# A retention layer and a swish MLP on one core: all crossbar transposes on the SyncE queue, batch 2's among them, and eight stores held back

## The chip, the core and the metric

The kernel runs on one core of a Trainium2 chip. Its time is the device time of one execution in microseconds (us). Times of single steps come from one profiled execution, counted from the start of its span.

## What is computed

Eight batches of eight heads (sequence 576, head size 64) go through a retention layer, attention without softmax whose scores are weighted by a decay per head, and then through an MLP with a swish whose slope beta is given per hidden unit.

```python
scores = (q @ k.T) / sqrt(64)                       # q, k, v: 8 x 8 x 576 x 64, float32
D      = where(i >= j, gamma[h] ** (i - j), 0)      # gamma[h] = 1 - 2 ** (-5 - h)
x      = ((scores * D) @ v)                         # heads side by side: 4608 x 512
h      = x @ w_in                                   # 512 x 2048
out    = (h / (1 + exp(-beta * h))) @ w_out         # 2048 x 512, out 4608 x 512 float32
```

## The kernel before

**Tiles.** A batch's first 512 rows are cut into four chunks of 128. The last 64 rows of two batches together make a tail tile of 128, so there are four of these. The list `seq` numbers the tiles in the order of their attention: 0 to 15 are the chunks of batches 0 to 3, 16 and 17 two tails, 18 to 33 batches 4 to 7, 34 and 35 the other two tails. The MLP works in blocks of 512 rows: block m below 8 holds the first 512 rows of batch m, block 8 all the tails.

**The order.** Everything is written in the order in which each engine is to run it. `fill` is a list of MLP steps: `up` (L406; 4 matmuls of 512 columns and a Silu on ScalarE) and `down` (L419; 4 matmuls and, after four of them, an eviction to `ot` by VectorE and a store on SyncE's DMA queue, called SP here, L436). `streams` are lists of attention steps with a due place each, and `merged` (L443) puts a step ahead of the first fill step whose number has reached its due place. `d0` = 16 and `u1` = 32 are the places where block 0's down projection and block 1's up projection begin; block 1's down projection begins at step 58; `base[2]` = 74 is the start of block 2's up projection, and each later block takes 32 steps.

**The attention of one tile.** `load_q` (L74) and `load_kv` (L85) fetch q of a batch, and k and v of one chunk, on SP. `load_kv(n)` counts chunks without the tails. `pre_q` (L237) scales q by the decay into `qs` in bf16, and `pre` (L251) casts k to `kn` (L273) and scales v to `vn` (L255); from batch 2 on all of these run on GpSimd. q and k must then be transposed, to `qT` and `kT`. Then `first` (L542) runs the state update `a_st` and the scores `a_sc` (L323, masked by VectorE into `R`), and `outputs` (L547) the products with v (L366), those with the state (L351) and the eviction `xT` that the up projection reads.

**Two kinds of transposes.** For batches below `XB`, `t_q` (L294) and `t_k` (L300) transpose on TensorE into PSUM tiles `T` and copy them out (L298, L304). From `XB` on, `x_q` (two for a batch), `x_k` (one for two chunks) and `x_tail` (one for a tail) call `turn` (L280), a crossbar transpose by DMA from SBUF to SBUF. Before the change `turn` issues on ScalarE's queue. The due places of all of these are made in the lists of L527 to L539 for the first chunks, and by `pair_prep` (L553) for the others; the loop of L572 gives each pair of chunks the place `at` of its `first`.

An issue on SP or ScalarE waits for the data and the buffers it needs, and what stands behind it on the same engine waits too. Every DMA also takes one of eight semaphores in turn, shared between the two queues, so that a ninth is issued only when the first of them has landed.

Of the kernel before, what the change touches and what calls it, by code (L numbers as in the profile page):

```python
# [19 lines left out]
def kernel(  # L20
# [10 lines left out]
    nc = tc.nc  # L31
# [9 lines left out]
    CB = MB // P  # L41
# [25 lines left out]

    NQ = 6
    E = CB
    XB = 3  # L70
    QB = 2
    q_tiles, kv_tiles = {}, {}

# [204 lines left out]
        return t[:, 2 * p:2 * p + 2, :].rearrange("p h d -> p (h d)")  # L278

    def turn(dst, src):  # L280
        nc.scalar.dma_start_transpose(dst.rearrange("p j pr s -> p (j pr) s"), src.rearrange("p j h d -> p (j h d)"))

    def x_q(b, u):
        turn(batch[b]["qT"][:, 2 * u:2 * u + 2], batch[b]["qs"][:, 2 * u:2 * u + 2])

    def x_k(b, u):
        kn, kT = pair[b, u]
        turn(kT, kn)

    def x_tail(i):  # L290
        turn(live[i]["qkT"], live[i]["qk"])
# [122 lines left out]
                             start=(ko == 0), stop=(ko == KO - 1))  # L414
        nc.scalar.activation(gts[m][:, fo, :, w], ph, ACT.Silu, scale=beta_sb[:, fo:fo + 1])  # L415

    pos_, ots = {}, {}

    def down(m, ms, f0, fn=4, n0=0, nn=d_model):  # L419

        gT = gts[m]
        if f0 == 0:
            pos_[ms] = psum.tile([P, d_model], F32, name="po", tag="mm", bufs=3)
        po = pos_[ms]
        for fo in range(f0, f0 + fn):
            nc.tensor.matmul(po[:, :nn], gT[:, fo, ms, :], w_out_sb[:, fo, n0:n0 + nn],  # L426
                             start=(fo == 0), stop=(fo == FO - 1))
        if f0 + fn < FO:
            return
        if ms == 0:  # L430
            ots[m] = stage.tile([P, MB // P, d_model], F32, name="ot", tag="wt", bufs=4)
        ot = ots[m][:, ms, n0:n0 + nn]
        nc.vector.tensor_copy(ot, po[:, :nn])  # L433
        if m < B:
            rows = out[m * S:m * S + MB].rearrange("(s i) n -> s i n", i=CB)
            nc.sync.dma_start(rows[:, ms, n0:n0 + nn], ot)  # L436
        else:
            for x in range(2):
                r0 = (2 * ms + x) * S + MB
                nc.sync.dma_start(out[r0:r0 + TL, n0:n0 + nn], ot[x * TL:(x + 1) * TL])  # L440
# [12 lines left out]
    def F(f, *a):  # L453
        return lambda: f(*a)
# [49 lines left out]
    fill = [F(up, 0, fo) for fo in range(FO)]  # L504
    d0 = len(fill)
    fill += [F(down, 0, ms, f0) for f0 in range(0, FO, 4) for ms in range(3)]
    fill += [F(down, 0, 3, f0) for f0 in range(0, FO, 4)]

    u1 = len(fill)
    fill += [F(up, 1, fo, 2 * x, 2) for x in range(2) for fo in range(10)]  # L510
    fill += [F(up, 1, fo) for fo in range(10, FO)]
    fill += [F(down, 1, ms, f0) for ms in range(MB // P) for f0 in range(0, FO, 4)]
    base = {1: u1 + 10}
    for n, m in enumerate(blocks[2:], 2):
# [6 lines left out]
    def second(i):  # L521
        for f in (a_O, lambda j: a_cross(j, False), a_x):
# [6 lines left out]
               [(d0 - 4 + 3.3 * g, F(cast_w_out, g)) for g in range(WG)],  # L529
               [(10.3, F(load_q, 1))] + [(10.3, F(load_kv, CB + n, (j,))) for n, j in keys_first],  # L530
               [(10.4, F(load_q, 2))] + [(10.4, F(load_kv, 2 * CB + n)) for n in range(2)],
               [(d0 + 8.6, F(load_kv, 2 * CB + 2)), (d0 + 10.1, F(load_kv, 2 * CB + 3))],
               [(d0 + 7, F(pre_q, 1, n)) for n in range(4)] + [(d0 + 10.6, F(t_q, 1, 0)), (d0 + 12.6, F(t_q, 1, 1))],
               [(d0 + 8, F(pre, 4, (0,))), (d0 + 8, F(pre, 5, (0,))), (d0 + 9, F(pre, 4, (1,))), (d0 + 9, F(pre, 5, (1,))),
                (d0 + 12.7, F(t_k, 4)), (d0 + 12.8, F(t_k, 5)), (d0 + 13.8, F(a_sc, 4)), (d0 + 13.81, F(a_sc, 5)),
                (d0 + 14.8, F(a_st, 4)), (d0 + 15.9, F(second, 4))],
# [16 lines left out]
    def pair_prep(i, at):  # L553
        b, c = seq[i]
        if b is None:
            return [(at - 31, F(load_tail, c)), (at - 21.5, F(pre, i)), (at - 21, F(load_tail, c + 1)),
                    (at - 13, F(pre, i + 1)), (at - 12, F(x_tail, i)), (at - 9.5, F(x_tail, i + 1))]
        n, st = full.index(i), []
        if b < XB:
            if c == 0:  # L560
                st += [(at - 12 + x, F(pre_q, b, x)) for x in range(4)]
                st += [(at - 5.5, F(t_q, b, 0)), (at - 4.5, F(t_q, b, 1))]
                st += [(at - 6.5 + x / 2, F(pre, i + x)) for x in range(CB)]
            return st + [(at - 3.5, F(t_k, i)), (at - 2.5, F(t_k, i + 1))]
        if c == 0:
            st += [(at - 30, F(load_q, b))] + [(at - 20 + x, F(pre_q, b, x)) for x in range(4)]
            st += [(at - 14 + 1.5 * x, F(x_q, b, x)) for x in range(2)]
        return st + [(at - 28, F(load_kv, n)), (at - 26, F(load_kv, n + 1)), (at - 16, F(pre, i)),
                     (at - 15, F(pre, i + 1)), (at - 10.5, F(x_k, b, c // 2))]

    todo = list(range(2 * CB, len(seq), 2))
    for n in range(1, B - 1):  # L572

        take = [i for i in todo if seq[i][0] == n + 1 or n == B - 2 or seq[i] == (None, 0) and n == CB - 1]
        todo = todo[len(take):]
        lo, hi = (base[n] + 11, base[n + 1] - 12) if n == 1 else (base[n] + 3, base[n + 1] - 8)
        at = [lo + x * (hi - lo) / (len(take) - 1) for x in range(len(take))]
        if len(take) == 2 and n > 1:
            at[1] -= 6
        for i, t in zip(take, at):  # L580
            st = pair_prep(i, t) + [(t, F(first, i))]
            if seq[i][0] is None:
                st.append((t + 5, F(second, i)))
            elif seq[i][1] == 0:
                st.append((t + 2, F(a_st, i + 1)))
            else:
                st.append((t + 5, F(outputs, i - 2)))
            streams.append(st)
# [32 lines left out]
```

## Time and profile before

| | |
|---|---|
| time, median of 3 runs | 311.74 us (311.5 to 311.76) |
| the profiled execution: time, span | 311.92 us, 310.1 us |
| TensorE matmuls busy | 298.5 us, 96% |
| ScalarE, VectorE, GpSimd busy | 143.0, 106.9, 96.0 us |
| SP's DMA queue | 46.15 MB, 61.5% of the DMA engines' span |
| ScalarE's DMA queue | 6.30 MB, 13.6% of it |
| clock granted to TensorE | 0.998 |

The span runs from the first to the last instruction; the profiled execution's time is 1.8 us longer. Busy time is the time in which an engine has at least one instruction running. The share of a DMA queue is the time that its packets took, as a share of the span of all 16 DMA engines; where packets overlap, the sum in a short window can pass 1.

### The profile page before, as it was taken

Reading aid. Unit: us, or ns where it says so; the run is one execution under the profiler, and the core shown is the slowest. Engines: PE = TensorE matmul, PEld = TensorE weight load, DVE = VectorE, ACT = ScalarE, POOL = GpSimd, SP = SyncE. Lnnn points to the kernel's source line nnn. Section 1 sums busy time; section 2 is a strip of 40 time slices with the busy share of each in tenths; the row PEclk is TensorE's granted clock in tenths of the full one; section 3 lists DMA queues with packets and bytes.
Section 4 is the critical chain, followed back from the end, with each engine's and each line's share of the span. In section 5 each row is a group of like instructions: output and inputs, shape, how many; then the busy total and the mean of one; then the engine's idle time right before and its main releaser. Section 6 shows DMA issues by size and latency. Waiting matters only on the chain.

```text
span 310.1 us, 5363 instructions
## 1 busy us (share of the span) xinstructions
PE 298.5 (96%) x2144; PEld 157.8 (51%) x2177; DVE 106.9 (34%) x191; ACT 143.0 (46%) x256; POOL 96.0 (31%) x131
## 2 busy tenths in 40 slices
PE   7789999999999999999999999999999999999995
PEld 5544456775544454454554545455545444444444
DVE  7554476342531342434430434043405420010012
ACT  5567626995138412560186117711673037207700
POOL 4663026846524282254308031902420000000000
PEclk9999999999999999999999999999999999999999
DMA  8999999998989999999897697968852110031011
GB/s 207 221 355 387 380 232 273 233 257 179 202 197 162 224 189 235 218 212 198 133 234 107 136 205 207 201 115 192 196 76 37 68 70 0 17 88 34 0 70 68
DMA packets 123897, 52.79 MB, mean 170 GB/s; under 512 B 105680, under 2 KB 116320, under 8 KB 123872
## 3 DMA queue, kind: packets, MB, share of 16 engines
q1 hardware_dynamic: 98496, 46.15, 61.5%
q10 hardware_dynamic: 25376, 6.30, 13.6%
q8 instruction: 17, 0.28, 0.4%
q14 instruction: 8, 0.07, 0.1%
HBM read 36.71 MB, written 9.44 MB: 149 GB/s over the span
## 4 chain that ended last, share of the span: by engine, by line
PE 85%; DMA 6%; SPq 5%; DVE 1%; issue 1%; ACT 1%; POOL 1%; POOLq 0%
PE po L426 40%; PE ph L413 35%; DMA wt<-in_moe_w_in_dram 4%; SPq L94 3%; PE O L366 3%; PE sc L323 3%; DMA qn<-in_q_dram 2%; PE O L351 2%; PE st L396 2%; SPq L178 1%; POOL qs L247 1%; PE T L297 1%; PE T L303 1%; ACT gT L415 0%; DVE xT L384 0%
## 5 line engine op out<-in xcount | busy, mean ns | idle before, releaser
L415 ACT ACTIVATE gT<-ph,beta_sb 128x512 bf16<-128x512 f32 (+1 forms) x154 | 99.2, 659 | 86.3 <-PE ph L413 83.4
L413 PE MATMUL ph<-xT,w_in_sb 128*128 128x512 bf16 (+1 forms) x600 | 129.3, 365 | 3.2 <-DVE w_in_sb L186 0.9
L426 PE MATMUL po<-w_out_sb,gT 128*128 128x512 bf16 (+2 forms) x591 | 126.7, 368 | 1.1 <-issue 0.3
L413 PEld LDWEIGHTS <-w_in_sb 128*128 128x128 bf16 x616 | 58.7, 98 | 65.0 <-DVE w_in_sb L186 2.3
L426 PEld LDWEIGHTS <-gT 128*128 128x128 bf16 x608 | 57.1, 98 | 62.5
L333 DVE TENSOR_TENSOR R<-sc,causal 128x512 bf16<-128x512 f32 x71 | 44.3, 684 | 68.9 <-PE sc L323 68.9
L433 DVE COPY ot<-po 128x512 f32<-128x512 f32 (+2 forms) x38 | 25.0, 662 | 92.1 <-PE po L426 92.0
L255 POOL TENSOR_TENSOR vn<-kvn,gv 128x512 bf16<-128x512 f32 x32 | 33.4, 1042 | 22.8 <-DMA kvn<-in_v_dram 11.5
L247 POOL TENSOR_TENSOR qs<-qn,gq 128x512 bf16<-128x512 f32 x24 | 24.3, 1042 | 33.2 <-DMA qn<-in_q_dram 33.2
L273 POOL CAST kn<-kvn 128x512 bf16<-128x512 f32 x32 | 19.6, 612 | 47.7 <-DMA kvn<-in_k_dram 47.3
L401 ACT CAST sbd<-st 64x256 bf16<-64x256 f32 x48 | 17.4, 362 | 15.0 <-PE st L396 14.3
L384 DVE CAST xT<-O 128x512 bf16<-128x512 f32 x24 | 15.8, 688 | 19.6 <-PE O L366 9.6
L384 ACT CAST xT<-O 128x512 bf16<-128x512 f32 x11 | 6.4, 586 | 32.2 <-PE O L351 25.2
L396 PE MATMUL st<-vn,kn 128*128 128x128 bf16 x128 | 12.4, 219 | 0.2 <-POOL vn L255 0.2
L396 PEld LDWEIGHTS <-kn 128*128 128x128 bf16 x128 | 9.3, 98 | 5.0 <-issue 0.2
L366 PE MATMUL O<-R,vn 128*64 128x128 bf16 x288 | 10.7, 221 | 0.0
L323 PE MATMUL sc<-qT,kT 64*128 64x128 bf16 x256 | 10.3, 217 | 0.4 <-ACT kT L304 0.2
L366 PEld LDWEIGHTS <-vn 128*64 128x64 bf16 x288 | 8.5, 110 | 4.1 <-issue 3.6
L323 PEld LDWEIGHTS <-kT 64*128 64x128 bf16 x288 | 8.1, 94 | 3.8 <-ACT kT L304 1.5
L304 ACT COPY kT<-T 128x512 bf16<-128x512 bf16 x12 | 6.9, 586 | 4.8 <-PE T L303 4.8
L208 PE MATMUL ph<-warm 128*128 128x128 f32 (+1 forms) x24 | 7.0, 429 | 1.2 <-DVE warm L119 1.2
L186 DVE CAST w_in_sb<-wt 128x256 bf16<-128x256 f32 (+1 forms) x14 | 6.0, 476 | 5.2 <-DMA wt<-in_moe_w_in_dram 5.2
(56 smaller groups left out, 90.2 us busy)
## 6 DMA issues: line engine op xcount, KB each, us to landing
qn<-in_q_dram SPq DMA_DIRECT2D x16, 512.0 KB, 5.8
kvn<-in_k_dram SPq DMA_DIRECT2D x32, 256.0 KB, 5.9
kvn<-in_v_dram SPq DMA_DIRECT2D x32, 256.0 KB, 5.6
out_dram<-ot SPq DMA_DIRECT2D x31, 256.0 KB, 2.7
wt<-in_moe_w_out_dram SPq DMA_DIRECT2D x4, 1024.0 KB, 9.5
wt<-in_moe_w_in_dram SPq DMA_DIRECT2D x4, 512.0 KB, 7.5
wt<-in_moe_w_in_dram SPq DMA_DIRECT2D x2, 1024.0 KB, 11.8
out_dram<-ot SPq DMA_DIRECT2D x9, 128.0 KB, 2.4
```

Of the source, the lines that this page charges most:

```text
L247: e.tensor_tensor(batch[b]["qs"][:, cs, hs], q_tiles[b][:, hs, cs].rearrange("p h i d -> p i h d"), gq[:, cs, hs].unsqueeze(3).to_broadcas ...
L255: nc.gpsimd.tensor_tensor(live[i]["vn"][:], kv_tiles.pop(i)[:, 1], gains(gv, c), ALU.mult)
L273: nc.gpsimd.tensor_copy(kn[:, c % 2], t[:, 0])
L323: nc.tensor.matmul(view(sc[j][:, p, :]), L["kT"][r, p, :], rhs, start=True, stop=True, skip_group_check=True)
L333: nc.vector.tensor_tensor(R[:, j], sc[j][:], causal4[:] if i == CB - 1 else m_b, ALU.mult)
L366: nc.tensor.matmul(O[j * D:(j + 1) * D, p, :], vn[:, 2 * p + j, :], R[:, j, p, :], start=p == 0 and not (early and crossed), stop=early or ...
L384: (nc.scalar.copy if on_act else nc.vector.tensor_copy)(x, O[:])
L396: nc.tensor.matmul(st[:, p, :], heads(L["kn"], p), heads(L["vn"], p), start=(c == 0 and p == 0), stop=True, skip_group_check=True)
L413: nc.tensor.matmul(ph, w_in_sb[:, ko, fo * P:(fo + 1) * P], xts[m][:, ko, :, w], start=(ko == 0), stop=(ko == KO - 1))
L415: nc.scalar.activation(gts[m][:, fo, :, w], ph, ACT.Silu, scale=beta_sb[:, fo:fo + 1])
L426: nc.tensor.matmul(po[:, :nn], gT[:, fo, ms, :], w_out_sb[:, fo, n0:n0 + nn], start=(fo == 0), stop=(fo == FO - 1))
L433: nc.vector.tensor_copy(ot, po[:, :nn])
```

## The change

`XB` goes from 3 to 2, so batch 2 is transposed by the crossbar as batches 3 to 7 are. `turn` issues on SP instead of ScalarE, for all 28 crossbar transposes. The stores of blocks 0 and 1 are kept in a list, and `release` issues four at 4.5 steps before `base[2]` and four at 8 steps after it. The due places around batch 2 move: its `first` steps from 53 and 62 to 58 and 64.5, its casts and scalings ahead of them, the third and fourth loads of its chunks, and the loads of batch 3's second half.

```diff
-    XB = 3
+    XB = 2
...
     def turn(dst, src):
-        nc.scalar.dma_start_transpose(dst.rearrange("p j pr s -> p (j pr) s"), src.rearrange("p j h d -> p (j h d)"))
+        nc.sync.dma_start_transpose(dst.rearrange("p j pr s -> p (j pr) s"), src.rearrange("p j h d -> p (j h d)"))
...
-    pos_, ots = {}, {}
+    pos_, ots, held = {}, {}, []
+
+    def release(n):
+        for _ in range(n):
+            nc.sync.dma_start(*held.pop(0))
...
-            nc.sync.dma_start(rows[:, ms, n0:n0 + nn], ot)
+            if m < 2:
+                held.append((rows[:, ms, n0:n0 + nn], ot))
+            else:
+                nc.sync.dma_start(rows[:, ms, n0:n0 + nn], ot)
...
-               [(d0 + 8.6, F(load_kv, 2 * CB + 2)), (d0 + 10.1, F(load_kv, 2 * CB + 3))],
-               [(d0 + 7, F(pre_q, 1, n)) for n in range(4)] + [(d0 + 10.6, F(t_q, 1, 0)), (d0 + 12.6, F(t_q, 1, 1))],
+               [(d0 + 8.6, F(load_kv, 2 * CB + 2)), (d0 + 12.6, F(x_q, XB, 0)), (d0 + 12.7, F(x_q, XB, 1)),
+                (d0 + 13.6, F(x_k, XB, 0)), (d0 + 13.8, F(load_kv, 2 * CB + 3)),
+                (base[2] - 4.5, F(release, 4)), (base[2] + 8, F(release, 4))],
+               [(d0 + 7, F(pre_q, 1, n)) for n in range(4)] + [(d0 + 12.5, F(pre_q, XB, n)) for n in range(4)] + [(d0 + 10.6, F(t_q, 1, 0)), (d0 + 12.6, F(t_q, 1, 1))],
...
-        if b < XB:
+        if b == XB:
             if c == 0:
-                st += [(at - 12 + x, F(pre_q, b, x)) for x in range(4)]
-                st += [(at - 5.5, F(t_q, b, 0)), (at - 4.5, F(t_q, b, 1))]
-                st += [(at - 6.5 + x / 2, F(pre, i + x)) for x in range(CB)]
-            return st + [(at - 3.5, F(t_k, i)), (at - 2.5, F(t_k, i + 1))]
+                return [(d0 + 13, F(pre, i + x, (0,))) for x in range(2)] + \
+                       [(d0 + 14, F(pre, i + x, (1,))) for x in range(2)]
+            return [(u1 + 8 + x / 2, F(pre, i + x)) for x in range(2)] + [(u1 + 18.5, F(x_k, b, 1))]
...
-        return st + [(at - 28, F(load_kv, n)), (at - 26, F(load_kv, n + 1)), (at - 16, F(pre, i)),
+        early = b == XB + 1 and c > 0
+        return st + [(at - (25.4 if early else 28), F(load_kv, n)), (at - (25.3 if early else 26), F(load_kv, n + 1)), (at - 16, F(pre, i)),
...
-        lo, hi = (base[n] + 11, base[n + 1] - 12) if n == 1 else (base[n] + 3, base[n + 1] - 8)
+        lo, hi = (base[n] + 16, base[n + 1] - 9.5) if n == 1 else (base[n] + 3, base[n + 1] - 8)
```

On SP the issue order around batch 2 becomes: `load_kv(10)`; `x_q(2, 0)`, `x_q(2, 1)`, `x_k(2, 0)`; `load_kv(11)`; `load_q(3)`; `load_kv(12)`; `x_k(2, 1)`; `load_kv(13)`; `x_q(3, 0)`, `x_q(3, 1)`, `x_k(3, 0)`; `load_kv(14)`, `load_kv(15)`; the four stores of block 0; the loads of the first tail; `x_k(3, 1)`; the four stores of block 1; the loads of the second tail.

## The prediction

> **What bounds the kernel now.** I read the page's span and busy line first, then the chain of waits, then the timelines of ScalarE, of SyncE's DMA queue (SP) and of GpSimd around the third batch (batch 2).
>
> ```profile
> span 310.1 us, 5363 instructions
> PE 298.5 (96%) x2144; PEld 157.8 (51%) x2177; DVE 106.9 (34%) x191; ACT 143.0 (46%) x256; POOL 96.0 (31%) x131
> ```
>
> TensorE is busy for all but 11.6 us. The table by stages of 10 us puts 4.7 us of that into the first 20 us and 3.2 us into the last 10, where the change touches nothing. In between TensorE runs matmul behind matmul at 0.216 us per 512 columns, so whatever leaves its queue shortens the kernel, if nothing new makes it wait. The chain of waits from 60 to 78 us shows what leaves (start, length, what):
>
> ```profile
> 62.24 0.45 PE T L297 x8
> ...
> 63.12 0.45 PE T L297 x8
> ...
> 64.00 0.22 PE T L303 x4
> ...
> 64.76 0.22 PE T L303 x4
> ...
> 72.40 0.39 PE T L303 x4
> ...
> 73.65 0.22 PE T L303 x4
> ```
>
> These are batch 2's transposes through PSUM, t_q twice and t_k four times, all on the chain. (The 0.39 stands beside a step of the down projection that shows 3 of its 4 matmuls; a fourth at 0.22 leaves 0.22 for the transposes.) One real gap lies in the middle, seen in the timeline from 155 to 167 us (start, length, engine; in brackets the idle time before):
>
> ```profile
> 162.17 2.29 ACTq L281 DMA_TRANSPOSE kT<-kn  x1
> 164.50 2.49 ACT L415 ACTIVATE gT<-ph,beta_sb 128x512 bf16<-128x512 f32 x4 [1.73 <-POOL qs L247]
> 165.24 2.10 PE L413 MATMUL ph<-xT,w_in_sb 128*128 128x512 bf16 x9 [0.60 <-ACT gT L415]
> ```
>
> A crossbar transpose held ScalarE's queue for 2.29 us, the Silu behind it was late, the PSUM tiles of the up projection ran out, and TensorE stood for 0.60 us.
>
> **Part 1, removed.** TensorE loses 2 x 8 transposes of t_q and 4 x 4 of t_k: 2 x 0.45 + 4 x 0.22 = 1.78 us of the chain. The evictions go with them (ScalarE 1.01 + 4 x 0.58 us, VectorE 0.69 us). They lay beside matmuls and are worth nothing of themselves, but they matter as a check: from 60 to 64 us ScalarE is busy 4.00 of 4.00 us, so if it kept its load TensorE would wait for it instead. In 62 to 66 us it loses 1.01 + 2 x 0.58 = 2.2 us where TensorE loses 1.34, so it does not become the bound. I count -1.78.
>
> The Trainium skill (VectorE: DVE Perf Modes, The three transpose paths) gives 390 ns for a 128x128 transpose on TensorE and 1309 ns on the DMA crossbar, and its rules say to use TensorE where the result may go to PSUM, which speaks against this change. As an estimate by that page the 32 transposes would be worth 12.5 us and the kernel would take 298.8 us; the trace's spacing of 0.056 us in a full queue decides, and the sum below goes by it.
>
> **Part 2, moved.** The other 24 transposes leave ScalarE for SP. ScalarE no longer stops for an issue (1.25 us at least, 3.51 us at most), and the gap of 0.60 us has no cause left: -0.60. The other stops cost TensorE nothing that the stage table shows, since its idle time there is 0.05 to 0.16 us per 10 us.
>
> **Part 3, what SP takes on.** 28 transposes of at least 1.25 us are 35 us of issuing. The Trainium skill (DMA: Bandwidth & Descriptors, Issuing engines are not separate DMA queues) says that a second issuing engine only saves issue time, as all run on the same DMA engines; no run here shows the two against each other yet. SP waits in order: a transpose that waits for GpSimd (L247, L273) holds every load behind it. Later on there is room. SP stood for 120.2 us in the stores of line 436 waiting for VectorE's ot, so it reaches a transpose behind a store about when that block's down projection does. The closest I find is batch 4's x_k(4,0): behind the store of block 2's last slice (122.06 us before, about 119.7 after) and two x_q it issues at 123, lands after 5.6 us (median) at 128.6, and is needed by first(18) at 134.7 - 2.4 = 132.3. Batch 7's x_k(7,0), 210 + 5.6 against 218.5, is as close. Both at nothing by the median; 0.8 us late for the former at the longest landing, 10.1 us.
>
> The tight place is batch 2. SP's rows of before, GpSimd's rows, the DMA queue from 56 to 76 us, and the transposes' own rows (issue ns min/median/max, then landing):
>
> ```profile
> 56.49 1.11 SPq L94 DMA_DIRECT2D kvn<-in_k_dram  x1
> 57.65 1.07 SPq L94 DMA_DIRECT2D kvn<-in_v_dram  x1
> 58.81 1.46 SPq L436 DMA_DIRECT2D out_dram<-ot  x2
> 60.36 0.42 SPq L94 DMA_DIRECT2D kvn<-in_k_dram  x1
> ```
> ```profile
> 55.17 4.04 POOL L247 TENSOR_TENSOR qs<-qn,gq 128x512 bf16<-128x512 f32 x4 [2.40 <-DMA qn<-in_q_dram]
> ...
> 65.45 0.61 POOL L273 CAST kn<-kvn 128x512 bf16<-128x512 f32 x1 [1.57 <-DMA kvn<-in_k_dram]
> ...
> 72.84 4.04 POOL L247 TENSOR_TENSOR qs<-qn,gq 128x512 bf16<-128x512 f32 x4 [4.37 <-DMA qn<-in_q_dram]
> ```
> ```profile
> q1 hardware_dynamic: 12006, 4.71, 100.2%
> ```
> ```profile
> L281 ACTq DMA_TRANSPOSE kT<-kn x14: 1247/1288/3514, 80.0 to 233.1; - x14
> DMA to landing us min/median/max: 3.0/5.6/10.1
> ```
>
> The stores at 58.81 and 61.83 are replaced by x_q, x_q, x_k of batch 2, ahead of load_kv(11). Their inputs are there: qs ends at 59.2, two kn casts of 0.61 make 60.4. SP is free at 58.7, so the three issue at 58.8, 60.05 and 61.3. The x_k lands at 61.3 + 5.6 = 66.9. Its user first(8) has moved from step 53 to 58. Step 58 began at 71.70; without the 1.34 us of transposes and without first(8) and a_st(9) ahead of it (0.99) it begins at 69.4, the scores at 69.6: 2.7 us to spare, or 1.8 late at 10.1.
>
> x_k(2,1) is the narrow one. It needs load_kv(11), now behind three transposes instead of two stores. A transpose holds the DMA engines for 13.6% of 310.1 / 24 = 1.76 us, a 256 KB transfer in this full stretch for 1.1 us (4.71 MB in 20 us), so that load lands 3 x 1.76 - 2 x 1.1 = 3.1 us later: cast done at 65.45 + 3.1 + 0.61 = 69.1, transpose issued then. first(10)'s scores come at 69.6 + 0.55 + 0.22 + 7 x 0.864 + 0.22 = 76.6. At the median the transpose lands at 74.7, in time. If it must wait until everything ahead of it has drained (q of batch 3 lands at 72.84 + 3 x 1.76 - 4 x 1.1 = 73.7, two loads 2.2, itself 1.76) it lands at 77.7, 1.1 late. At 10.1 us it is 2.6 late. Below nothing is excluded: TensorE has no earlier gap there to close. I take 0.5, between the median row and the drained queue, because the rows are ScalarE's own ring and the new transposes stand in the loaded one.
>
> **Part 4, stores held.** The eight stores of blocks 0 and 1 go out after steps 69.5 and 82, near 83 and 91 us. Only blocks 4 and 5 take their buffers again (there are four), after 150 us, so nothing waits for them. They meet the tail loads there; the DMA engines are filled 1.25 from 80 to 88 us but 0.70 from 88 to 92, and pre(16) has over 10 us before its scores. At nothing; if that cover fails, the bound is x_k(3,1), which then lands past 96 against first(14) at 103.5.
>
> **Sum.** The profiled execution took 311.92 us, 0.18 over the median. 311.92 - 1.78 - 0.60 + 0.5 = 310.04, less 0.18 is **309.9 us**.
>
> **The rivals.** (a) *Late transposes, slower.* If crossbar transposes in SP's full ring land like the worst row (10.1 us), x_k(2,0) costs 1.8 us, x_k(2,1) 2.6 - 1.8 = 0.8 more at least, and x_k(4,0), with the same landing and a deadline 2.6 later, nothing; issues of 3.51 instead of 1.25 us on the three transposes ahead add 6.8 us to x_k(2,1)'s place, of which the wait for its cast covers none, so 2.6 to 9.4 us in all. Half way, 6 us, gives 315.4; the lower end 311.9. It makes the kernel slower once the stalls exceed 3.0 us. For it: the queue is 100.2% full there. Against: the median lands 4.5 us earlier, and four stores leave that stretch. (b) *Eaten up, no change.* The stalls come to 1.8 to 3.0 us, 2.4 in the middle, as when x_k(2,1) lands 9.9 us after its issue: 309.4 + 2.4 = 311.8. (c) *ScalarE's gap stays*, because TensorE then waits for something else there: 310.5, still faster.
>
> **How the numbers follow.** A measurement of this kernel can tell about 0.2%, 0.62 us, from no change. Forecast with (c), stalls below 1.76 us: 0.70. (b): 0.14. (a): 0.16. No stall at all gives 309.4; a few gaps of 0.05 us that close with it reach 309.0, the low end. The high end goes through (b) into the foot of (a), 312.6, and leaves out most of (a) and a little below.
>
> **What would show it.** Right: no T rows after 55 us but batch 1's, 32 matmul records fewer, TensorE's busy time down by 1.8 us, no Silu after 150 us that waits over 1 us behind a transpose, SP rows of line 281 with about 1.25 us each, and scores (L323) of batch 2 at about 69.6 and 76.6 us with under 1 us idle before them. Wrong: idle time of TensorE in front of L323 or L351 released by a DMA of kT or qT, or L273 waiting for loads so long that a later first() stands still.

## The result and the profile after

The changed kernel takes 309.35 us (median of 6 runs, 308.81 to 310.62) where the kernel before, run beside it, takes 311.62 us. The ratio is 0.9929, 95% interval 0.9913 to 0.9946: faster by 2.27 us. The forecast was 309.9 us, faster.

The profiled execution took 309.26 us. The page's span and busy line:

```profile
span 307.6 us, 5289 instructions
...
PE 297.1 (97%) x2112; PEld 156.5 (51%) x2145; DVE 106.0 (34%) x190; ACT 141.6 (46%) x251; POOL 96.6 (31%) x131
```

TensorE has 32 matmul records fewer and 1.4 us less busy time, and the span is 2.5 us shorter. The two totals do not split the gain, because 0.9 us of the idle time that went lies in the first 20 us (4.71 us before, 3.82 after), which the change does not touch. The starts of the same matmuls split it better. Block 1's up projection begins 0.12 us earlier than before (52.10 us instead of 52.22), block 2's 2.00 us earlier (86.70 instead of 88.70), and block 4's down projection 2.88 us earlier (166.68 instead of 169.56). TensorE's timeline around batch 2's scores (L323), where idle time would stand in brackets:

```profile
68.89 0.39 PE L396 MATMUL st<-vn,kn 128*128 128x128 bf16 x4
69.20 0.62 PE L323 MATMUL sc<-qT,kT 64*128 64x128 bf16 x16
69.76 1.69 PE L430 MATMUL po<-w_out_sb,gT 128*128 128x512 bf16 x7
...
76.03 0.39 PE L396 MATMUL st<-vn,kn 128*128 128x128 bf16 x4
76.35 0.62 PE L323 MATMUL sc<-qT,kT 64*128 64x128 bf16 x16
76.91 4.49 PE L430 MATMUL po<-w_out_sb,gT 128*128 128x512 bf16 x19
...
157.18 8.15 PE L413 MATMUL ph<-xT,w_in_sb 128*128 128x512 bf16 x37
```

There are no brackets: both crossbar transposes had landed when their scores were due. The last row is the stretch of block 4's up projection in which the gap of 0.60 us had been; the matmuls now run through. SP's queue in the same two places (line 281 is `turn`):

```profile
59.12 3.36 SPq L281 DMA_TRANSPOSE qT<-qs  x2
62.57 1.43 SPq L281 DMA_TRANSPOSE kT<-kn  x1
...
69.75 3.69 SPq L281 DMA_TRANSPOSE kT<-kn  x1
...
155.64 4.55 SPq L281 DMA_TRANSPOSE kT<-kn  x1
```

The last row is x_k(5, 1), the transpose that had held ScalarE for 2.29 us. On SP it takes 4.55 us to issue, and TensorE does not wait: the loads behind it have time, the Silus did not. The transposes' own rows, for the comparison with ScalarE's ring:

```profile
L281 SPq DMA_TRANSPOSE kT<-kn x16: 1231/1777/5349, 62.6 to 226.1; - x16
DMA to landing us min/median/max: 3.0/4.8/7.7
```

An issue got dearer (median 1.78 us instead of 1.29 for k, 1.45 instead of 1.28 for q). The landings show no common delay: k's came sooner (median 4.8 us instead of 5.6) and q's later (4.1 instead of 3.5). The Trainium skill (DMA: Bandwidth & Descriptors, Issuing engines are not separate DMA queues) says that DMAs run on the same 16 DMA engines whichever engine started them, so that a second issuing engine saves only the time of the issue, usually small beside the DMA. The landings do not contradict the first part. The issue is not small here, at up to 5.35 us against landings of 3.0 to 7.7 us, and the first experiment shows what it costs on ScalarE.

### The profile page after: what moved, and what is told of

The parts are those of the page before. It is cut to its first block, busy times and chain, and to the rows that moved or that the text cites. A ratio compares the mean times of both kernels' runs of the same rounds, so it can differ in the third digit from the quotient of the medians.

```text
span 307.6 us, 5289 instructions
## 1 busy us (share of the span) xinstructions
PE 297.1 (97%) x2112; PEld 156.5 (51%) x2145; DVE 106.0 (34%) x190; ACT 141.6 (46%) x251; POOL 96.6 (31%) x131
## 4 chain that ended last, share of the span: by engine, by line
PE 88%; SPq 4%; DMA 4%; issue 1%; DVE 1%; ACT 0%
PE po L430 40%; PE ph L413 38%; DMA wt<-in_moe_w_in_dram 4%; SPq L94 3%; PE sc L323 3%; PE O L366 3%; PE st L396 2%; PE O L351 2%; SPq L178 1%; DVE xT L384 0%; DVE w_in_sb L186 0%; PE O L348 0%; SPq L81 0%; PE T L297 0%; ACT sbd L401 0%
## 5 line engine op out<-in xcount | busy, mean ns | idle before, releaser
L323 PE MATMUL sc<-qT,kT 64*128 64x128 bf16 x256 | 10.3, 217 | 0.3 <-ACT kT L304 0.2
L262 POOL TENSOR_TENSOR kn<-tln,gq 128x512 bf16<-128x512 f32 x4 | 4.2, 1044 | 18.9 <-DMA tln<-in_q_dram 13.6
L323 PEld LDWEIGHTS <-kT 64*128 64x128 bf16 x288 | 8.1, 94 | 3.6 <-ACT kT L304 1.1
```

Source lines behind the costliest of these rows:

```text
L323: nc.tensor.matmul(view(sc[j][:, p, :]), L["kT"][r, p, :], rhs, start=True, stop=True, skip_group_check=True)
```

## The experiments

**Who issues.** The changed kernel with all transposes on ScalarE again, batch 2's placed where their inputs are ready.

```diff
-        nc.sync.dma_start_transpose(...)
+        nc.scalar.dma_start_transpose(...)
...
-               [(d0 + 8.6, F(load_kv, 2 * CB + 2)), (d0 + 12.6, F(x_q, XB, 0)), (d0 + 12.7, F(x_q, XB, 1)),
-                (d0 + 13.6, F(x_k, XB, 0)), (d0 + 13.8, F(load_kv, 2 * CB + 3)),
+               [(d0 + 8.6, F(load_kv, 2 * CB + 2)), (u1 + 10.5, F(x_q, XB, 0)), (u1 + 12, F(x_q, XB, 1)),
+                (u1 + 13.5, F(x_k, XB, 0)), (d0 + 13.8, F(load_kv, 2 * CB + 3)),
...
-            return [(u1 + 8 + x / 2, F(pre, i + x)) for x in range(2)] + [(u1 + 18.5, F(x_k, b, 1))]
+            return [(u1 + 8 + x / 2, F(pre, i + x)) for x in range(2)] + [(u1 + 25, F(x_k, b, 1))]
```

> The changed kernel with turn() back on ScalarE's queue for all 28 transposes; batch 2's are given due places at which their inputs are ready (x_q at u1 + 10.5 and u1 + 12, x_k at u1 + 13.5 and u1 + 25), all else as changed, stores held too. My theory (TensorE bound; moving the issue off ScalarE is what makes room): the 1.78 us of TensorE transposes stay away, but four issues of 1.25 to 3.5 us now stand between the Silus of 58 to 70 us, where ScalarE is busy 8.7 of 10 us, and the later gap near 165 us (0.60 us) returns: 309.35 + 0.6 + 1 to 4 = 311 to 314 us, with idle time of TensorE at L413 released by ScalarE's Silu. Rival (the gain comes from fewer TensorE instructions and held stores alone, whoever issues): 309.3 to 309.9 us.

Measured: 318.13 us (317.16 to 319.12), ratio to the kernel before 1.0192, interval 1.0171 to 1.0213. TensorE's timeline:

```profile
62.06 0.60 PE L413 MATMUL ph<-xT,w_in_sb 128*128 128x256 bf16 x4 [0.69 <-ACT gT L415]
63.98 1.03 PE L413 MATMUL ph<-xT,w_in_sb 128*128 128x256 bf16 x8 [1.32 <-ACT gT L415]
68.58 3.15 PE L413 MATMUL ph<-xT,w_in_sb 128*128 128x256 bf16 x13 [3.57 <-ACT gT L415]
...
113.49 0.62 PE L323 MATMUL sc<-qT,kT 64*128 64x128 bf16 x16 [1.36 <-DMA kT<-kn]
```

and ScalarE's, with the issue that made the longest of these waits:

```profile
63.56 4.45 ACTq L281 DMA_TRANSPOSE kT<-kn  x1
...
68.06 1.21 ACT L415 ACTIVATE gT<-ph,beta_sb 128x256 bf16<-128x256 f32 x3 [3.77 <-issue]
```

The main mechanism is the expected one, idle time of TensorE behind Silus that stand behind a transpose's issue: 0.69 + 1.32 + 3.57 = 5.6 us of it. The size is not: I had allowed 4 us. Two costs came on top, a wait of 1.36 us for a transpose of k at 113.49 us and a lower clock, which a later experiment tells apart from the wait before it. The gap near 165 us, expected to return, did not. The rival, that it doesn't matter who issues, falls. With these due places, batch 2 on the crossbar is a loss on ScalarE and a gain on SP; no other places were run on ScalarE.

**The move alone.** The kernel before with that one word changed.

```diff
-        nc.scalar.dma_start_transpose(...)
+        nc.sync.dma_start_transpose(...)
```

> The kernel before with one word changed: turn() issues on SyncE's queue; XB stays 3, no store is held, no due place moves. My theory: only the gap of 0.60 us near 165 us closes, so 311.62 - 0.60 = 311.0 us, TensorE's busy time unchanged near 298.5 us. Rival (SyncE waits in order, so a transpose that waits for GpSimd holds loads and a later first() stalls): 312 us or more, with idle time at L323. Second rival (most of the change's gain was ScalarE's relief): below 310.3 us.

Measured: 311.11 us (310.59 to 312.25) against 311.68; ratio 0.9983, interval 0.9971 to 0.9995. That is 0.57 us where 0.60 was expected; the interval allows 0.2 to 0.9. In the trace the stretch from 155 to 167 us has no gap, and no wait at L323 appears. The rivals, a stall of a later `first` and a larger relief, fall. What is left to the changed kernel is 311.11 - 309.35 = 1.76 us (1.70 when each is taken against the kernel before that ran beside it).

**The price of a transpose on TensorE.** The changed kernel with 64 idle ones.

```diff
+    def idle_turns(n, tag):
+        T = psum.tile([P, 8, P], BF16, name="T", tag=tag, bufs=3 if tag == "mm" else 2)
+        for i in range(n):
+            nc.tensor.transpose(T[:, i, :], ident[:], ident[:])
+
+    streams.append([(u1 + 16 + x, F(idle_turns, 8, "sc")) for x in range(8)])
```

> The changed kernel with 64 transposes of the identity on TensorE added, eight ahead of each of the steps 48 to 55 of the fill; their result is never read and nothing else moves. It measures the price of the term that the change removed. My theory (a transpose in a full queue costs its spacing in the chain, 0.45 / 8 = 0.056 us): 64 x 0.056 = 3.6 us, 309.35 + 3.6 = 312.9 us, TensorE's busy time up by as much. Rival 1 (the page's 390 ns for one transpose): 64 x 0.39 = 25 us, about 334 us. Rival 2 (transposes hide in gaps of the up projection, where ScalarE's Silus set the pace): 309.4 to 310.5 us.

Measured: 312.75 us (312.70 to 312.99), 3.40 us above the changed kernel, 0.053 us each (0.050 when each is taken against the kernel before that ran beside it). The chain of waits shows them as it showed those of the kernel before:

```profile
62.28 0.45 PE T L554 x8
62.72 0.44 PE ph L413 x4
63.16 0.45 PE T L554 x8
```

The 390 ns that the Trainium skill gives (VectorE: DVE Perf Modes, The three transpose paths) is not what a transpose costs here between other matmuls; nor do transposes hide in the up projection. With 32 of them, 1.6 to 1.7 us, this agrees with the 1.76 us that the move alone left.

**The stores held back.** The changed kernel with all eight stores issued at once, then with only block 0's held.

```diff
-            if m < 2:
+            if m < 0:
...
-                (d0 + 13.6, F(x_k, XB, 0)), (d0 + 13.8, F(load_kv, 2 * CB + 3)),
-                (base[2] - 4.5, F(release, 4)), (base[2] + 8, F(release, 4))],
+                (d0 + 13.6, F(x_k, XB, 0)), (d0 + 13.8, F(load_kv, 2 * CB + 3))],
```
```diff
-            if m < 2:
+            if m < 1:
...
-                (base[2] - 4.5, F(release, 4)), (base[2] + 8, F(release, 4))],
+                (base[2] - 4.5, F(release, 4))],
```

> The changed kernel with the stores of blocks 0 and 1 issued at once, as before; three of block 0's then stand ahead of x_q(2, 0) on SyncE's queue and the fourth behind load_kv(11). My theory (the transposes of batch 2 are in time by little): x_k(2, 0), issued at 62.6 us in the changed kernel, slips by three stores of 1.1 us of the DMA engines and lands about 1 us after the 69.2 us at which its scores are due; x_k(2, 1) slips by 3 to 4.4 us and is 1 to 2.5 us late: 310.3 to 312 us in all. Rival (holding the stores is idle, the queue has the room): 309.4 us, no idle time at L323.

> The changed kernel with only block 0's four stores held; block 1's are issued when their rows are ready, among batch 3's transposes. With the run that held none (314.88 us) it tells which four cost the time. My theory: block 0's stood ahead of load_kv(11) and x_k(2, 1), whose landing sets TensorE's wait at tile 10; block 1's come behind it and batch 3's transposes have 4 us or more to spare, so 309.3 to 309.9 us and no wait at L323 above 0.5 us. Rival (any store that waits for its rows holds the transposes behind it): 311 us or more, with a wait at the scores of batch 3 or at the tails.

Measured: 314.88 us without any held (311.84 to 316.38; ratio 1.0084, interval 1.0048 to 1.0120), and 309.23 us with block 0's alone (308.92 to 309.37; ratio 0.9917, interval 0.9899 to 0.9936). Block 0's four stores are the whole of it; holding block 1's changes nothing that can be measured. Both rivals fall: holding stores is not idle, and block 1's do not hold up the transposes behind them enough to cost time. Without any held, SP and TensorE show:

```profile
59.50 1.95 SPq L443 DMA_DIRECT2D out_dram<-ot  x3
...
73.93 3.69 SPq L281 DMA_TRANSPOSE kT<-kn  x1
```
```profile
80.00 1.04 PE L323 MATMUL sc<-qT,kT 64*128 64x128 bf16 x16 [3.56 <-DMA kT<-kn]
80.96 5.62 PE L430 MATMUL po<-w_out_sb,gT 128*128 128x512 bf16 x19
```

x_k(2, 1) went out 4.2 us later than in the changed kernel (73.93 instead of 69.75), and tile 10's scores waited 3.56 us for it; I had expected 1 to 2.5. x_k(2, 0), expected about 1 us late, was in time. The rows after the wait tell more: 16 score matmuls take 1.04 us instead of 0.62, and 19 of the down projection 5.62 instead of 4.49.

**The wait and the clock.** The same kernel with 16 idle matmuls where TensorE stood idle.

```diff
+    def keep_busy(n):
+        T = psum.tile([P, MB], F32, name="T", tag="sc", bufs=2)
+        for _ in range(n):
+            nc.tensor.matmul(T[:], ident[:], w_in_sb[:, 0, :MB], start=True, stop=True, skip_group_check=True)
...
     def first(i):
         a_st(i)
+        if i == 2 * CB + 2:
+            keep_busy(16)
```

> The run without held stores once more, with 16 idle matmuls of 512 columns on TensorE (16 x 0.216 = 3.5 us) ahead of the scores of tile 10, where that run stood idle for 3.56 us; nothing else differs and their result is never read. That run's times fell into two groups, 311.8 to 312.7 us at a mean granted clock of 0.999 to 1.0 and 314.5 to 316.4 us at 0.989 to 0.993. My theory (the wait itself costs about 3 us, and the rest is a lower granted clock that follows it, 0.59 from 80 to 84 us): with TensorE busy through the wait the clock stays at 1.0 and all runs fall at 312 to 313.3 us. Rival (the upper group waits longer for the transpose, and the clock is a mere companion): the median stays at 314 us or above and runs above 315 us remain.

Measured: 312.81 us (312.29 to 313.73), clock 0.998 to 1.0 in all eight runs. The stage tables of the run without held stores, and of this one (columns: stretch, TensorE, its weight loads, VectorE, ScalarE, GpSimd busy, granted clock, DMA share, GB/s):

```profile
76.00:80.00 4.00, 0.44 (x7) 0.22 (x5) 0.00 (x0) 0.73 (x2) 3.07 (x4) 0.99 1.25 205
80.00:84.00 4.00, 3.88 (x24) 1.95 (x26) 3.08 (x5) 0.00 (x0) 4.00 (x5) 0.59 1.25 258
```
```profile
76.00:80.00 4.00, 4.00 (x33) 1.89 (x32) 0.00 (x0) 0.73 (x2) 3.56 (x4) 1.00 1.29 213
80.00:84.00 4.00, 3.84 (x28) 1.89 (x24) 3.08 (x5) 0.00 (x0) 3.58 (x5) 1.00 1.35 184
```

x_k(2, 1) goes out at 73.46 us, about as late as without the idle matmuls (73.93). They fill the wait, and the runs above 314 us are gone, so the rival, a longer wait in the upper group, falls. The 5.5 us of the run without held stores are then a wait of some 3 us (312.2 us in its four runs at a clock of 0.999 or 1.0) and, in the six others, up to 4 us of lower clock behind it (316 us at 0.989). Only one of these runs left a trace, so the length of the wait in the others is not measured.

**The scores' places.** The changed kernel with batch 2's `first` at its old places.

```diff
-        lo, hi = (base[n] + 16, base[n + 1] - 9.5) if n == 1 else (base[n] + 3, base[n + 1] - 8)
+        lo, hi = (base[n] + 11, base[n + 1] - 12) if n == 1 else (base[n] + 3, base[n + 1] - 8)
```

> The changed kernel with batch 2's first() at the old due places, 11 steps behind base[1] and 12 ahead of base[2] (steps 53 and 62 instead of 58 and 64.5). The scores are then due at about 64.9 and 74.2 us, and where TensorE waits for them it shows when the transposes land. My theory: x_k(2, 0) is issued at 62.6 and lands 3.0 to 7.7 us later, so TensorE stands for 1 to 4 us ahead of the scores of tile 8, and for up to 1.5 us more ahead of tile 10: 310.5 to 314 us. Rival (crossbar transposes land within 3 us even in a full queue, and the move of first() buys nothing): 309.4 us.

Measured: 312.55 us (311.00 to 314.58), ratio 1.0023, interval 1.0003 to 1.0042; the profiled execution took 311.78. TensorE's timeline, and SP's row of the transpose it waits for:

```profile
67.10 0.62 PE L323 MATMUL sc<-qT,kT 64*128 64x128 bf16 x16 [2.33 <-DMA kT<-kn]
```
```profile
62.59 1.55 SPq L281 DMA_TRANSPOSE kT<-kn  x1
```

x_k(2, 0) lands 4.5 us after its issue, and TensorE waits 2.33 us for it; tile 10 hardly waits. Moving the first pair's `first` by five steps is what turns the crossbar's delay into no wait at all. The rival, that the move buys nothing, falls.

## Why the prediction was right, and where its sizes were off

*Part 1*, 1.78 us: the changed kernel stands 1.76 us below the move alone, the 64 idle transposes give 32 x 0.053 = 1.7 us, and the timelines gain 2.00 - 0.12 = 1.88 us between 52 and 89 us. The sign that TensorE's busy time falls by 1.8 us failed (1.4 us), since the first 20 us show 0.9 us more of it than before. The estimate of 298.8 us does not follow the prediction's own sum: with 12.5 us in the place of 1.78 the sum gives 299.1 us.

*Part 2*, 0.60 us: the move alone gave 0.57, with the gap near 165 us gone from its trace. The sign that the rows of line 281 stay at about 1.25 us each failed: on SP they had medians of 1.78 us for k and 1.45 for q. TensorE's timeline shows no wait that came of it.

*Part 3*, the tight place. The times worked out for it were close: load_kv(11)'s cast was to begin at 65.45 + 3.1 = 68.5 and began at 68.47; x_k(2, 1) was to issue at 69.1 and did at 69.75; the scores were due at 69.6 and 76.6 and ran at 69.20 and 76.35. The term that was mis-sized is the stall, taken at 0.5 us and measured at none: with it left out the sum gives 309.4, and 309.35 was measured. That the two agree so closely is partly luck, for the timelines gain 0.1 us more than forecast in part 1 and some 0.2 us more at the gap, and the end of the span, from the last matmul on, is 0.4 us longer than before. The trace has x_k(2, 1) by itself:

```profile
L281 SPq DMA_TRANSPOSE kT<-kn x1: 3686/3686/3686, 69.8 to 69.8; - x1
DMA to landing us min/median/max: 6.0/6.0/6.0
```

It landed at 69.75 + 6.0 = 75.7 us, about 0.6 us ahead of its scores: later than the median row said (74.7) and earlier than the drained queue (77.7). The loads ahead of it had indeed all landed first, v of the last one at 67.86 + 7.0 = 74.9, but two sizes of that step were too large. It took batch 3's q to land 0.9 us later than before, since three transposes had replaced four stores; GpSimd in fact began on it at 72.73, as early as before (72.84). And it gave the transpose 1.76 us behind the last load, where it took 0.9.

*Part 4*, the stores: rightly put at nothing after the move. Part 3 had counted their transfers out of the tight stretch, at 1.1 us each, but the prediction has no price for leaving them there. Left in place, block 0's cost 5.6 us, from 309.23 to 314.88.

*Rival (a)* had the right place, x_k(2, 1) behind a full queue, and the stores show it. Its price lacked the clock: it counted the wait alone, and without held stores the kernel lost 2.9 us in its runs at full clock and up to 7.0 in the others. Its issues of 3.51 us did occur (3.69 us for x_k(2, 1)), but not on the three transposes ahead of it. *Rivals (b) and (c)* did not occur: batch 2's scores did not wait, and ScalarE's gap went.

## What to carry to other kernels

When the matrix engine runs without gaps, price its small instructions by their spacing in the chain, not by their latency, and move them off if the replacement can land before its user; then move the user back until it does. A DMA issue belongs on an engine whose queue nobody waits for: a transpose that takes 4.55 us to issue costs TensorE nothing on SP, and another, of 4.45 us on ScalarE, cost it 3.57 us. Stores whose result nobody needs could be taken out of a full stretch of the DMA queue here at no measurable cost; hold only those that stand ahead of the tight transfer.

## What was not expected of the hardware

A single wait of TensorE can cost twice. After 3.56 us without matmuls the granted clock was 0.59 in the next 4 us; filling the wait with idle matmuls kept it at 1.00. With the transposes on ScalarE it was 0.79, 0.50 and 0.86 in the three stretches of 4 us from 64 to 76 us. There the fall came within the last wait and not at its end, as the stretches of one microsecond show (columns as in the stage tables above):

```profile
65.00:66.00 1.00, 0.01 (x1) 0.00 (x0) 0.00 (x0) 0.00 (x0) 0.00 (x0) 1.00 1.35 224
66.00:67.00 1.00, 0.00 (x0) 0.00 (x0) 0.00 (x0) 0.00 (x0) 0.00 (x0) 0.65 1.14 265
67.00:68.00 1.00, 0.00 (x0) 0.00 (x0) 0.00 (x0) 0.00 (x0) 0.97 (x1) 0.50 1.15 230
```

The Trainium skill (TensorE: Matmul & The Clock Gate, Part 1: The HAM clock gate) says that the clock falls to half after an idle window of about 3.4 us, and that the window runs freely. The wait of 3.56 us fits this. A window that may begin at any time would also explain why some runs of one kernel kept a clock of 1.0 and others had 0.989, though no run shows that. The run with the transposes on ScalarE does not fit: when its clock fell, after 66 us, the last wait (from 65.0 us) had lasted less than 2 us, and TensorE had worked for 1.03 us just before it. So a lower clock also came of waits shorter than the window that stood close together. In the run with early scores the profiled execution waited 2.33 us and kept a clock of 1.0, while six other runs had 0.989 or 0.994; how long those waited is not in any trace, so whether one such wait alone can lower the clock stays open.

Little idle time is left between the first 30 us and the last matmul: 0.16, 0.34, 0.17 and 0.16 us at 48, 52, 56 and 143 us. No run tried to close these gaps. Holding only block 0's stores is as fast as the change, and simpler.
